# Splitting a tile's new weights: all quarters on VectorE, one per tick, instead of two on VectorE and two on GpSimd

## The chip, the cores and the metric

One core of a Trainium2 chip. The metric is the time of one execution in microseconds of the device; a time of a kernel is the median of several executions.

## The reference

Three layers over 10112 tokens (2 sequences of 5056) of width 256. The first is a linear recurrence along each sequence, the other two are mixtures of 8 experts of which each token takes one.

```python
# recurrence, per channel
log_a = 8 * sigmoid(r_gate) * log(clip(sigmoid(a_param)))
a = exp(log_a);  g = sqrt(max(1 - a*a, 1e-6)) * sigmoid(i_gate) * x
h[t] = a[t] * h[t-1] + g[t]
# mixture of experts; the second layer has no modality bias
logits = x @ w_gate + modality_bias[modality_id]
e = argmax(logits);  gate = softmax(logits)[e]
out = gate * (max(x @ w1[e], 0) @ w2[e])      # w1 256 x 1024, w2 1024 x 256
```

## The kernel before

**Tiles and slots.** A layer's tokens are sorted by expert: each is given a row number and GpSimd scatters its row to memory by an indirect DMA (`scatter`, L217). A *tile* is 256 rows of one expert. The program has a fixed sequence of *slots*, one tile each: slots 0 to 39 are layer 1, slots 40 and later layer 2. Which expert a slot's tile has, and whether its weights differ from those that its weight set holds, is worked out on the chip in tables (`plan_steps`) and read from there by each engine as a register (`entry`).

**Arithmetic.** TensorE takes 32-bit numbers in a form that holds only part of their digits, so every operand stands as two parts, high and low: `w1h, w1l, w2h, w2l` for weights, `xh, xl` for the tile's rows, `hTh, hTl` for the hidden layer. A product is three matmuls: high by high, low by high, high by low (`ffn1`, L898 to L900; `ffn2`, L912 to L914). ScalarE makes `hTh` (L902), VectorE `hTl` (L903).

**Ticks.** A slot is 6 ticks (`POINTS`): `ffn1` in ticks 0 to 3, `ffn2` in ticks 4 and 5. The main loop (L1110 to L1152) issues a tick's matmuls and then, in turn with one another, the steps that the agenda holds for that tick: chunks of the recurrence (`chunk_at`, layer 1 only), the routing (`pick`, `rank`), the list of a later phase's tiles (`plan_steps`), and what follows the slot before (`end_steps`). Every engine runs its own queue in program order.

**Weights.** There are two sets of weights on chip, which slots use in turn. SyncE loads a later slot's w1 and w2 as four quarters of 128 x 1024 into buffers named `stage` (`load_weights`, L798 to L817). `split` (L857 to L881) makes two parts of a quarter: ScalarE copies it to the high part (L863), then the difference is taken as the low part (L864) by the engine that a letter names, V for VectorE and G for GpSimd. Quarters 0 and 1 are w1, 2 and 3 are w2. In layer 1 a small fifth piece, `stagew` (128 x 64, always VectorE), holds columns that give the second layer's routing. All of it is under a condition (`when`, a test and a jump on each engine that takes part) on the table's entry `f2`, except in the first two slots of a layer, whose weights always change. A slot of which the condition holds is called a *reload* here.

```python
POINTS = 6
SPLIT = (4, 4, 5, 5)                     # tick in which each quarter of the next slot's weights is split
BY = ('VVVG', 'VVGG', 'VVGG')            # engines: first tile, slot 0, other slots
parts = [i for i in range(4) if SPLIT[i] == point]                      # in the main loop
split(nxt, *parts, *([4] if 3 in parts and t else []), by=BY[1 if t == 0 else 2])
```

So both w1 quarters are split behind the last hTl of a slot, in tick 4, and both w2 quarters in tick 5. `maybe_steps` (L1041 to L1080) holds the slots of layer 1 that may stay empty, as a nest of conditions; VectorE's test for the first of them is at L1063. `other_gates` (L847 to L855) has a jump at L852.

Of the kernel before, what the change touches and what calls it, by code (L numbers as in the profile page):

```python
# [16 lines left out]
P = 128  # L17
E = 8
# [4 lines left out]
T = 256  # tokens of a tile  # L23
H = T // P
CH = 512  # steps of the scan in a chunk
W = D + 2  # a row for a layer: token, its number, its gate
WR = D + E
GP = 128  # columns of the products with the second layer's gates
BIG = float(1 << 22)
CUTS = (1, 2, 3, 4, 6, 8)  # chunks of the scan after which tiles are listed  # L30
SW_QUEUES = 8
POINTS = 6  # ticks of a slot
SPLIT = (4, 4, 5, 5)  # ticks of a slot in which the quarters of the next one's weights are split
AHEAD = 11  # ticks from a chunk's loads to its start
T0 = 45
START = (5, 15, 34)
GATE = (3, 5)  # ticks of the first slot at which the gates of its and the next one's experts are worked out
FIRST = (37, 38, 45, 46)  # ticks of the splits of the first tile's weights
LOAD2 = T0 + 4
PACE = 12  # ticks between chunks, at least  # L40
NPH = 3
BIAS = 1
# Ticks of a chunk's steps, from its start: for the first, the second, the third, and the rest.
# [23 lines left out]
LISTS = (4, 4, 4, 4, 8)  # ticks that the phases' lists take  # L67
LATE = 4
BY = ('VVVG', 'VVGG', 'VVGG')  # engines that split the weights' quarters, of the first slots and the others
WARM = ((0, 'r', 1, 4, 2), (0, 'i', 1, 8, 2), (0, 'q', 1, 10, 3))  # products that keep TensorE's clock up: chunk, what they read, tick, how many  # L70
ALIGN = (0, 5)  # tick of a slot at which a chunk starts
# [10 lines left out]
def token_tiles(B, S):  # L82
    """Chunks of the scan (first step, steps, first token tile, token tiles), and the token tiles:
    lists of (sequence, first step, steps)."""
    chunks, tiles = [], []
    s = 0
    while s < S:
        w = min(CH, S - s)
        mine = []
        for b in range(B):  # L90
            for j in range(w // P):
                mine.append([(b, s + j * P, P)])
        rest = w % P
        if rest:
            assert rest * B == P
            mine.append([(b, s + w - rest, rest) for b in range(B)])
        chunks.append((s, w, len(tiles), len(mine)))
        tiles += mine
        s += w
    return chunks, tiles  # L100


LEAD = 4  # slots between the second layer's first list and its first tile


def phases(B, S):
    """How the tiles of both layers are cut into phases: (layer, routed chunks or slots that a
    phase's list rests on, slots, slots that are always run, last of the layer, first slot among
    those that are always run). Whatever the experts' shares, n routed tokens fill
    (n - E (T - 1)) / T tiles; the first phases have slots for as many as two experts' shares fill,  # L110
    and a slot that finds no tile runs on padding."""
# [6 lines left out]
    full = 0  # tiles done for certain  # L118
# [22 lines left out]
def positions(slots, filled, t):  # L141
    """Places in a phase's list, slot by slot: two runs side by side, as there are two sets of
    weights on chip; slots that may stay empty come last."""
    evens = len([i for i in range(filled) if (t + i) % 2 == 0])
    n = [0, evens]
    res = []
    for i in range(filled):
        res.append(n[(t + i) % 2])
        n[(t + i) % 2] += 1
    return res + list(range(filled, slots))  # L150


def shape_consts(B, S):
    """Arrays that depend on the shapes alone."""
# [20 lines left out]
def pair(a):  # L175
    """The two halves of a token tile's logits, innermost."""
    return bass.AP(a.tensor, a.offset, [list(a.ap[0]), [1, E], [D + E, 2]])


def scan_moe_moe2(tc, xT, rT, iT, apar, mod, mbias, wg1, wg2, wA1, wB1, wA2, cst_d, ids_d, tab_d, out):  # L180
# [11 lines left out]
    with ExitStack() as st:  # L192
# [12 lines left out]
        # Rows that experts get are written once, each to a place of its own, and read by tiles of  # L205
        # later phases: the accesses to them need no order but that of a phase behind its writes.
# [69 lines left out]
        # 4 * log(clip(sigmoid(a))): half of the decay's factor  # L276
# [19 lines left out]
        # the modality's bias of every token, by exact selection  # L296
# [17 lines left out]
        # rows that pad an expert's last tile: zeros, with a token number out of range  # L314
# [3 lines left out]
        # ... and a tile of them, for slots that find none  # L318
# [7 lines left out]
        def weave(a, b):  # L326
            """Two lists of steps as one, evenly."""
# [11 lines left out]
        def pick(lg, n, mk):  # L339
            """Of logits lg [P, n, E], in steps: the one-hot of the first maximum (bf16), and the  # L340
            softmax's value there."""
# [15 lines left out]
        def rank(oh, n, bs, mk, place):  # L357
            """In steps: the row numbers of n tiles' tokens behind `bs`, which moves on past them."""
# [33 lines left out]
        def at(tick, f, early=False):  # L392
            """Has a step done at a tick, among those of TensorE before the tile's or among the rest."""
            agenda.setdefault(tick, ([], [], []))[0 if early else 1].append(f)

        def at_all(tick, f):
            """Has the steps that `f` returns done at a tick, in turn with others."""
            agenda.setdefault(tick, ([], [], []))[2].append(f)

        def chunk_at(ci, s, first):  # L400
            """A chunk's steps from tick s on; a step's inputs are there by then, so that it doesn't
            hold up its engine."""
# [95 lines left out]
            def warm(box_, n_):  # L498
                """Products that nobody needs, which keep TensorE's clock up while it waits for the scan."""
# [30 lines left out]
        done = {}  # L530
        tabs = {}
        have = cp.tile([1, E], F32, name="have")  # whether an expert's gates are known
# [3 lines left out]
        def plan_steps(pi):  # L536
            """Lists a phase's tiles: expert, first row, whether the weights change, whether there
            is one."""
# [154 lines left out]
        def fresh(pi):  # L693
            """Whether a phase finds other weights on chip than its layer's."""
            return pi == 0 or plans[pi][0] != plans[pi - 1][0]

# [1 line left out]
        main = [(pi, s) for pi, pl in enumerate(plans) for s in range(pl[3])]  # L698
        NS = len(main)
        xT_, hT, pos = {}, {}, {}  # L700

        class Ring:
            """Buffers that tiles take in turn. While `held`, those at hand go round, as what is done
            under a condition can't get tiles."""
# [30 lines left out]
        class Slot:  # L735
            """A place for one tile: its phase and its place there, its set of weights, its buffers."""

            def __init__(self, pi, s, ws, pool_, bufs, tag=""):
# [4 lines left out]
                self.v = None  # L743
# [3 lines left out]
            def t(self, n):  # L747
                """A tile of this slot, got when first asked for."""
# [26 lines left out]
        def guard(sl):  # L775
            """For what is done for a slot only if there is a tile for it."""
# [21 lines left out]
        def load_weights(sl, part, gates=True):  # L798
            wA = wA1 if sl.layer == 1 else wA2
            if part == 0:  # L800
                sl.ev = sl.entry(0, {ET.SP}, E - 1)
                sl.f = None if sl.always else sl.entry(1, {ET.SP}, 1)
            js = {0: (0, 1), 1: (2, 3), 2: ()}[part]
# [19 lines left out]
        def gate(w, ps_, out):  # L823
            """w2  w_gate, of an expert whose w2 is in w, transposed."""
# [22 lines left out]
        def other_gates(sl):  # L847
            """All experts' gates, if a phase needs others than are known."""
# [7 lines left out]

        def split(sl, *parts, by=BY[2]):  # L857
            """Weights in two parts that TensorE takes in one pass each, a quarter at a time."""
# [20 lines left out]
            if 0 in parts and not sl.always:  # L879
# [36 lines left out]
        def end_steps(sl):  # L916
            """What follows a tile's products, in six parts."""
# [36 lines left out]
        slots = [Slot(pi, s, t % 2, mp, (3, 5)) for t, (pi, s) in enumerate(main)]  # L954

        # Ticks: those of the head, then POINTS of every slot. When chunks start: at the shortest
        # distance as long as there are no tiles, then in time for the lists that rest on them.
# [45 lines left out]
        def early(upto):  # L1003
            """The steps of TensorE at the tick before `upto`, and all before them."""
# [6 lines left out]
        def later(upto, *others):  # L1011
            """All steps of the ticks before `upto`, in turn with others."""
# [22 lines left out]
        for i, tick in enumerate(FIRST):  # L1035
            at(tick, lambda i=i: split(slots[0], i, by=BY[0]), early=True)
# [4 lines left out]
        def maybe_steps(pi):  # L1041
            """The first layer's slots that may stay empty, one by one: what is loaded for the first
            ahead of time, and all."""
# [38 lines left out]
        def tail(sl, nxt, nx2, rest):  # L1082
            """The second layer's slots that may stay empty, each with the start of the one behind."""
# [24 lines left out]
        prev = nest = None  # L1108
        todo = []
        for t, sl in enumerate(slots):  # L1110
# [8 lines left out]
            for point in range(POINTS):  # L1119
                early(tick(point))  # L1120
# [14 lines left out]
                if nxt:  # L1135
                    parts = [i for i in range(4) if SPLIT[i] == point]
                    if parts:
                        split(nxt, *parts, *([4] if 3 in parts and t else []), by=BY[1 if t == 0 else 2])
# [66 lines left out]
```

## Time and profile before

| | us |
|---|---|
| median of 3 runs | 1214.02 |
| lowest, highest run | 1210.79, 1217.70 |
| span of the profiled execution, first to last instruction | 1190.4 |
| TensorE busy in it | 1088.4 (91%), mean granted clock 0.962 |
| VectorE busy | 672.5 (56%) |
| ScalarE busy | 511.2 (43%) |
| GpSimd busy | 382.1 (32%) |

The profile is of one execution, whose own time from outside is not recorded; its span covers the instructions alone, and the medians contain what lies before and after them as well. PE is TensorE's matmuls, PEld its weight loads (in parallel with PE), DVE is VectorE, ACT ScalarE, POOL GpSimd, SP SyncE; a q behind an engine's name is its sequencer. "L864" is a line of the kernel before. Idle time of an engine is shown with what ended it.

### The profile page before, as it was taken

Reading aid. Unit: us, or ns where it says so; the run is one execution under the profiler, and the core shown is the slowest. Engines: PE = TensorE matmul, PEld = TensorE weight load, DVE = VectorE, ACT = ScalarE, POOL = GpSimd, SP = SyncE. Lnnn points to the kernel's source line nnn. Section 1 sums busy time; section 2 is a strip of 40 time slices with the busy share of each in tenths; the row PEclk is TensorE's granted clock in tenths of the full one; section 3 lists DMA queues with packets and bytes.
Section 4 is the critical chain, followed back from the end, with each engine's and each line's share of the span. In section 5 each row is a group of like instructions: output and inputs, shape, how many; then the busy total and the mean of one; then the engine's idle time right before and its main releaser. Section 6 shows DMA issues by size and latency. Waiting matters only on the chain. (4 is left out here: it accounts for less than half of the span.)

```text
span 1190.4 us, 26921 instructions
## 1 busy us (share of the span) xinstructions
PE 1088.4 (91%) x9112; PEld 1073.5 (90%) x9112; DVE 672.5 (56%) x1954; ACT 511.2 (43%) x817; POOL 382.1 (32%) x414
## 2 busy tenths in 40 slices
PE   4287889897999899989999799999999999999997
PEld 2287889897999899979999799999999999999997
DVE  6768778978686848555456643332434443333352
ACT  7735557546273525223234323332434542224362
POOL 2417341466241514241112421311333531113152
PEclk9688989998999989999999899999999999999999
DMA  7764464364333212151114233113332431113350
GB/s 248 236 226 147 169 180 134 109 215 162 114 113 108 96 46 74 41 140 50 37 55 140 77 119 120 43 50 108 122 108 73 141 120 47 45 53 106 124 171 26
DMA packets 69236, 133.76 MB, mean 112 GB/s; under 512 B 9740, under 2 KB 37395, under 8 KB 69042
## 3 DMA queue, kind: packets, MB, share of 16 engines
q1 hardware_dynamic: 57186, 100.19, 26.9%
q0 software_dynamic: 11856, 31.25, 7.4%
q8 instruction: 89, 1.46, 0.5%
q14 instruction: 105, 0.86, 0.2%
HBM read 95.49 MB, written 37.03 MB: 111 GB/s over the span
## 5 line engine op out<-in xcount | busy, mean ns | idle before, releaser
L912 PE MATMUL po<-w2h,hTh 128*128 128x256 f32 (+1 forms) x1344 | 396.1, 295 | 4.9 <-PEq L852 3.4
L898 PE MATMUL ph<-xh,w1h 128*128 128x256 f32 x1312 | 374.6, 286 | 26.8 <-DVEq L1063 7.9
L913 PE MATMUL po<-w2l,hTh 128*128 128x256 f32 (+1 forms) x1344 | 385.2, 287 | 1.1 <-DVE w2l L864 1.1
L914 PE MATMUL po<-w2h,hTl 128*128 128x256 f32 (+1 forms) x1344 | 384.7, 286 | 0.7 <-DVE hTl L903 0.7
L899 PE MATMUL ph<-xl,w1h 128*128 128x256 f32 x1312 | 370.1, 282 | 4.6 <-DVE xl L889 4.6
L900 PE MATMUL ph<-xh,w1l 128*128 128x256 f32 x1312 | 370.1, 282 | 1.2 <-DVE w1l L864 1.2
L903 DVE SCALAR_TENSOR_TENSOR hTl<-ph,hTh 128x512 fp32r<-128x512 f32 x336 | 231.2, 688 | 210.5 <-ACT hTh L902 208.9
L902 ACT ACTIVATE hTh<-ph 128x512 fp32r<-128x512 f32 x336 | 199.0, 596 | 321.7 <-PE ph L900 310.4
L898 PEld LDWEIGHTS ph<-xh,w1h 128*128 128x128 f32 x1312 | 252.4, 192 | 28.6 <-issue 15.6
L912 PEld LDWEIGHTS po<-w2h,hTh 128*128 128x128 f32 x1344 | 259.6, 193 | 3.6 <-issue 3.6
L913 PEld LDWEIGHTS po<-w2l,hTh 128*128 128x128 f32 x1344 | 259.5, 193 | 2.9 <-issue 1.6
L914 PEld LDWEIGHTS po<-w2h,hTl 128*128 128x128 f32 x1344 | 258.8, 193 | 1.1 <-DVE hTl L903 1.1
L899 PEld LDWEIGHTS ph<-xl,w1h 128*128 128x128 f32 x1312 | 250.5, 191 | 4.8 <-DVE xl L889 4.8
L900 PEld LDWEIGHTS ph<-xh,w1l 128*128 128x128 f32 x1312 | 249.8, 190 | 1.6 <-DVE w1l L864 1.6
L217 POOL DMA_INDIRECT out_dram<-orow,xr x88 | 86.5, 983 | 283.9 <-ACT orow L924 237.5
L924 ACT ACTIVATE orow<-po,xr 128x256 f32<-128x256 f32 x124 | 58.0, 472 | 274.8 <-PE po L914 272.6
L217 POOL DMA_INDIRECT X<-orow,rib x80 | 80.7, 1008 | 184.9 <-DVE rib L951 64.0
L864 POOL TENSOR_TENSOR w2l<-stage,w2h 128x1024 fp32r<-128x1024 f32 x37 | 93.3, 2542 | 127.8 <-ACT w2h L863 127.8
L929 DVE TENSOR_SCALAR orow<-po,xr 128x256 f32<-128x256 f32 x44 | 21.3, 484 | 148.8 <-PE po L914 148.8
L217 POOL DMA_INDIRECT X<-row,ria x79 | 88.4, 1119 | 23.6 <-issue 15.9
L459 PE MATMUL ps<-wI,it 128*128 128x136 f32 x280 | 49.0, 301 | 19.3 <-DVE it L438 15.5
L459 PEld LDWEIGHTS ps<-wI,it 128*128 128x128 f32 x280 | 39.8, 200 | 21.6 <-ACT rt L411 11.1
(171 smaller groups left out, 1044.1 us busy)
## 6 DMA issues: line engine op xcount, KB each, us to landing
stage<-in_wA SPq DMA_DIRECT2D x76, 512.0 KB, 4.6
xr<-X SPq DMA_DIRECT2D x84, 258.0 KB, 2.8
rt<-in_rT SPq DMA_DIRECT2D x18, 512.0 KB, 4.9
it<-in_iT SPq DMA_DIRECT2D x18, 512.0 KB, 5.5
xt<-in_xT SPq DMA_DIRECT2D x18, 512.0 KB, 4.7
X<-zr SPq DMA_DIRECT2D x17, 258.0 KB, 3.6
it<-in_wB SPq DMA_DIRECT2D x4, 512.0 KB, 7.8
out_dram<-orow,xr POOLq DMA_INDIRECT x88, 2.4
```

The costliest lines, as they stand in the source:

```text
L217: i = G.indirect_dma_start(out=dst, out_offset=bass.IndirectOffsetOnAxis(ap=idx, axis=0), in_=rows, in_offset=None, bounds_check=bound, oo ...
L459: PE.matmul(p[:, k * (P + E):(k + 1) * (P + E)], l[:, k, :], wI[:, k, :], start=True, stop=True)
L864: by.tensor_tensor(out=l, in0=src, in1=h.bitcast(F32), op=ALU.subtract)
L898: PE.matmul(p[:, j, :], h1[:, k, cs], sl.t("xh")[:, k, :], start=k == 0, stop=False)
L899: PE.matmul(p[:, j, :], h1[:, k, cs], sl.t("xl")[:, k, :], start=False, stop=False)
L900: PE.matmul(p[:, j, :], l1[:, k, cs], sl.t("xh")[:, k, :], start=False, stop=k == KD - 1)
L902: A.activation(hh[:], p[:], func=ACTF.Relu)
L903: V.scalar_tensor_tensor(out=hl[:], in0=p[:], scalar=0.0, in1=hh[:].bitcast(F32), op0=ALU.max, op1=ALU.subtract)
L912: PE.matmul(p[h][:, :wd], hh, h2[:, c, :wd], start=c == 0, stop=False)
L913: PE.matmul(p[h][:, :wd], hh, l2[:, c, :wd], start=False, stop=False)
L914: PE.matmul(p[h][:, :wd], hl, h2[:, c, :wd], start=False, stop=c == KF - 1)
L924: A.activation(orow[:, h, :D], p[h][:, :D], func=ACTF.Copy, scale=g1[:, h:h + 1])
```

## The change

All four quarters are split on VectorE; only the first tile of the program keeps its last quarter on GpSimd. The quarters go to ticks 2, 3, 4 and 5 of a slot, one each, where their loads were issued at least `LOADED` = 4 ticks before; otherwise to the ticks of before (`SPLIT_LATE`). For that, `load_weights` notes at which tick each half was issued. The table's entry `f2` is read at a slot's first split instead of at that of quarter 0. The rest of the diff takes comments away, so that line numbers of the changed kernel differ by a few.

```diff
-SPLIT = (4, 4, 5, 5)
+SPLIT = (2, 3, 4, 5)
+SPLIT_LATE = (4, 4, 5, 5)
+LOADED = 4
-BY = ('VVVG', 'VVGG', 'VVGG')
 ...
+        now = [-POINTS]
 ...
-                self.v = None
+                self.v = self.f2 = None
 ...
             if part == 0:
                 sl.ev = sl.entry(0, {ET.SP}, E - 1)
                 sl.f = None if sl.always else sl.entry(1, {ET.SP}, 1)
+                sl.came = {}
+            sl.came[part] = now[0]
 ...
-        def split(sl, *parts, by=BY[2]):
+        def split(sl, *parts, by='VVVV'):
 ...
-            if 0 in parts and not sl.always:
+            if sl.f2 is None and not sl.always:
                 sl.f2 = sl.entry(1, {ET.Activation, ET.DVE, ET.Pool}, 1)
 ...
-            at(tick, lambda i=i: split(slots[0], i, by=BY[0]), early=True)
+            at(tick, lambda i=i: split(slots[0], i, by='VVVG'), early=True)
 ...
             for point in range(POINTS):
+                now[0] = t * POINTS + point
 ...
-                    parts = [i for i in range(4) if SPLIT[i] == point]
+                    when_ = lambda i: SPLIT[i] if t * POINTS + SPLIT[i] >= nxt.came.get(i // 2, 1 << 20) + LOADED else SPLIT_LATE[i]
+                    parts = [i for i in range(4) if when_(i) == point]
                     if parts:
-                        split(nxt, *parts, *([4] if 3 in parts and t else []), by=BY[1 if t == 0 else 2])
+                        split(nxt, *parts, *([4] if 3 in parts and t else []))
```

How this moves instructions is seen best on VectorE. In its queue the number of tests on a register (COMPARE_AND_BRANCH) goes from 226 to 373, in ScalarE's from 233 to 380, in GpSimd's from 226 to 373; TensorE and SyncE keep theirs. The unconditional jumps are at the ends of the conditions' bodies.

VectorE in slot 3, from its last hTl on; w1l, w2l are the low parts, stage the loaded quarters, xl the next tile's rows, pbb the routing's; TENSOR_LOAD and ISA read the table's entry. Before:

```order
L903 SCALAR_TENSOR_TENSOR hTl<-ph,hTh 128x512
L889 TENSOR_TENSOR xl<-pt,xh 128x512
L773 TENSOR_LOAD tj_1016
L773 ISA x2
L787 COMPARE_AND_BRANCH
L864 TENSOR_TENSOR w1l_159<-stage,w1h_158 128x1024 x2
L787 UNCONDITIONAL_BRANCH x3
L787 COMPARE_AND_BRANCH
L864 TENSOR_TENSOR w2l_161<-stagew,w2h_160 128x8x8
L787 UNCONDITIONAL_BRANCH x3
L373 TENSOR_TENSOR pbb<-ph,base_152 128x16
```

With the change:

```order
L907 SCALAR_TENSOR_TENSOR hTl<-ph,hTh 128x512
L893 TENSOR_TENSOR xl<-pt,xh 128x512
L789 COMPARE_AND_BRANCH
L868 TENSOR_TENSOR w1l_159<-stage,w1h_158 128x1024
L789 UNCONDITIONAL_BRANCH x2
L789 COMPARE_AND_BRANCH
L868 TENSOR_TENSOR w2l_161<-stage,w2h_160 128x4x256
L789 UNCONDITIONAL_BRANCH x4
L789 COMPARE_AND_BRANCH
L868 TENSOR_TENSOR w2l_161<-stage,w2h_160 128x4x256
L868 TENSOR_TENSOR w2l_161<-stagew,w2h_160 128x8x8
L789 UNCONDITIONAL_BRANCH x2
```

One w1 quarter stands here instead of two, each w2 quarter follows under a test of its own, and the table's entry has been read earlier; pbb and what follows it come behind all of this.

VectorE in slot 12, from its third hTl to its last; the operations on gb, big, bg, dn are the routing's and the next list's. Before:

```order
L903 SCALAR_TENSOR_TENSOR hTl<-ph,hTh 128x512
L352 TENSOR_REDUCE gb<-exb 128x2
L605 TENSOR_SCALAR dn_4980<-exc 1x8
L353 TENSOR_SCALAR gb<-gb 128x2
L616 TENSOR_TENSOR big<-big,bg_4970 1x64
L354 RECIPROCAL gb<-gb 128x2
L609 SCALAR_TENSOR_TENSOR dn_4980<-dn_4980,av 1x8
L417 SCALAR_TENSOR_TENSOR it<-it,xt 128x512
L619 TENSOR_TENSOR bg_4970<-big,tab 1x64
L903 SCALAR_TENSOR_TENSOR hTl<-ph,hTh 128x512
L889 TENSOR_TENSOR xl<-pt,xh 128x512
```

With the change:

```order
L907 SCALAR_TENSOR_TENSOR hTl<-ph,hTh 128x512
L775 TENSOR_LOAD tj_3542
L775 ISA x2
L789 COMPARE_AND_BRANCH
L868 TENSOR_TENSOR w1l_163<-stage,w1h_162 128x1024
L789 UNCONDITIONAL_BRANCH x2
L353 TENSOR_REDUCE gb<-exb 128x2
L606 TENSOR_SCALAR dn_4998<-exc 1x8
L354 TENSOR_SCALAR gb<-gb 128x2
L617 TENSOR_TENSOR big<-big,bg_4988 1x64
L355 RECIPROCAL gb<-gb 128x2
L610 SCALAR_TENSOR_TENSOR dn_4998<-dn_4998,av 1x8
```

The table's entry is read here now, and the first w1 quarter stands ahead of all that leads to the last hTl of the slot.

## Rows read from the trace of the kernel before

**Rows 1.** The page, busy time by engine.
```profile
PE 1088.4 (91%) x9112; PEld 1073.5 (90%) x9112; DVE 672.5 (56%) x1954; ACT 511.2 (43%) x817; POOL 382.1 (32%) x414
```

**Rows 2.** Busy time by stretch: us, PE, PEld, DVE, ACT, POOL busy, PEclk, DMA share, GB/s.
```profile
157.00:272.00 115.00, 103.86 (x869) 102.17 (x868) 93.31 (x328) 63.19 (x95) 43.44 (x60) 0.93 0.49 157
...
677.00:1172.00 495.00, 494.31 (x4202) 493.73 (x4200) 196.36 (x304) 181.71 (x296) 143.59 (x111) 1.00 0.30 95
```

**Rows 3.** Waits of TensorE: us in total, times, longest.
```profile
PE ph L898 <- DVE hTl L903: 6.7, 3, 5.7
...
PE pt L887 <- DMA xr<-X: 0.5, 1, 0.5
```

**Rows 4.** The instructions of L864 on each engine: ns min/median/max, first and last start.
```profile
L864 DVE TENSOR_TENSOR w1l<-stage,w1h x38: 1199/1219/1227, 47.0 to 1157.2; 128x1024 fp32r<-128x1024 f32 x38
L864 POOL TENSOR_TENSOR w2l<-stage,w2h x37: 2339/2418/2947, 63.5 to 1160.6; 128x1024 fp32r<-128x1024 f32 x37
```

**Rows 5.** Timeline, end of slot 0: start, us, engine, line, instruction [idle before <-releaser].
```profile
72.29 0.39 PE L913 MATMUL po<-w2l,hTh 128*128 128x264 f32 x1 [1.10 <-DVE w2l L864]
```

**Rows 6.** Timeline from the end of slot 0, GpSimd and VectorE.
```profile
88.61 5.29 POOL L864 TENSOR_TENSOR w2l<-stage,w2h 128x1024 fp32r<-128x1024 f32 x2 [22.57 <-ACT w2h L863]
...
88.62 2.46 DVE L584 TENSOR_TENSOR big<-av,tab 1x64 f32<-1x64 f32 x1
...
91.85 2.06 DVE L590 TENSOR_TENSOR exc<-inc,av 1x8 f32<-1x8 f32 x1
...
96.07 0.68 DVE L903 SCALAR_TENSOR_TENSOR hTl<-ph,hTh 128x512 fp32r<-128x512 f32 x1
```

**Rows 7.** Timeline from the end of slot 3, GpSimd, VectorE and TensorE.
```profile
137.99 4.76 POOL L864 TENSOR_TENSOR w2l<-stage,w2h 128x1024 fp32r<-128x1024 f32 x2 [4.85 <-ACT w2h L863]
...
139.03 1.46 DVE L864 TENSOR_TENSOR w2l<-stagew,w2h 128x64 fp32r<-128x64 f32 x1 [1.75 <-ACT w2h L863]
...
140.82 2.01 DVE L378 TENSOR_TENSOR pb<-pb,oh 128x64 f32<-128x64 f32 x1
142.75 0.16 DVE L378 TENSOR_TENSOR pbb<-pbb,ohb 128x16 f32<-128x16 f32 x1
...
145.84 0.58 PE L898 MATMUL ph<-xh,w1h 128*128 128x256 f32 x1 [3.20 <-DVE cnt L561]
```

**Rows 8.** Busy time by stretch, columns as in the second group.
```profile
144.80:151.50 6.70, 5.66 (x26) 5.66 (x27) 6.56 (x32) 5.14 (x7) 5.47 (x6) 0.50 0.38 91
295.40:298.20 2.80, 2.80 (x13) 2.80 (x14) 2.68 (x12) 1.07 (x3) 0.99 (x1) 0.50 0.01 3
406.00:412.00 6.00, 4.69 (x38) 4.52 (x39) 5.86 (x28) 3.12 (x6) 3.48 (x4) 1.00 0.24 86
```

**Rows 9.** Timeline from the end of slot 12, VectorE and TensorE.
```profile
288.12 2.29 DVE L613 TENSOR_TENSOR dn<-dn,dn 1x8 f32<-1x8 f32 x1
...
291.02 2.35 DVE L628 TENSOR_TENSOR bg<-bg,big 1x64 f32<-1x64 f32 x1
...
295.29 0.55 PE L898 MATMUL ph<-xh,w1h 128*128 128x256 f32 x1 [5.71 <-DVE base L376]
```

**Rows 10.** Timeline at the end of slot 39, VectorE, ScalarE and TensorE.
```profile
653.56 2.08 DVE L378 TENSOR_TENSOR pbb<-pbb,ohb 128x16 f32<-128x16 f32 x1
...
655.88 2.04 DVE L951 TENSOR_TENSOR rib<-rb,vbb 128x2 int32<-128x2 f32 x1
...
655.34 0.47 ACT L924 ACTIVATE orow<-po,xr 128x256 f32<-128x256 f32 x1 [0.94 <-PE po L914]
...
663.22 0.55 PE L898 MATMUL ph<-xh,w1h 128*128 128x256 f32 x1 [7.92 <-DVEq L1063]
```

**Rows 11.** Timeline of VectorE in slot 11, behind a jump.
```profile
269.12 0.69 DVE L417 SCALAR_TENSOR_TENSOR it<-it,xt 128x512 f32<-128x512 f32 x1 [0.45 <-DVEq L787]
```

**Rows 12.** Timeline of GpSimd in slot 1, scatters.
```profile
103.27 1.91 POOL L217 DMA_INDIRECT X<-row,ria  x1 [0.30 <-issue]
105.48 0.97 POOL L217 DMA_INDIRECT X<-row,ria  x1 [0.30 <-issue]
```

More of the change, by code (lines that the diff above doesn't have):

```diff
@@ L1108, in scan_moe_moe2 @@
         prev = nest = None
+        now[0] = 0
         todo = []
```

## The prediction, made before the changed kernel was run

> **What bounds the kernel now.** I read the page first. TensorE is busy 91% of the span [rows 1], so time can be won only where TensorE stands still or runs at a lower clock. Next I read busy time by stretch: from 677 to 1172 us, nearly all of layer 2, TensorE is busy 494.31 of 495 us at a granted clock of 1.00 [rows 2], although eleven of the 18 reloads lie there. Nothing can be won in that stretch; what is added there must only stay hidden. The waits of TensorE put the rest before 677 us: 6.7 us in three waits for hTl, the longest 5.7 [rows 3], one of 5.71 for base [rows 9], one of 7.92 behind VectorE's sequencer at L1063 [rows 10]. What these have in common is seen in the timelines [rows 6, 7, 9, 10]: ahead of each, small VectorE operations last 2 us where their like last 0.15 to 0.2, exactly while GpSimd splits.
>
> So the question is what the six reloads of layer 1 (in slots 0, 1, 3, 10, 12 and 39) cost today through GpSimd, and what the same work costs on VectorE.
>
> **The prices.** A quarter takes 1.22 us on VectorE and 2.42 on GpSimd [rows 4]. GpSimd has 37, and keeps that of the first tile: 36 × 2.42 = 87 us leave it, and 36 × 1.22 = 44 us come to VectorE. In each reload VectorE gains two quarters, 2.4 us, and loses the lengthened operations. I take the reloads one by one. Every instant is one of the profiled execution, whose span is 1190.4 us; if its whole time is the median of the runs, 1214.0, then 23.6 us lie outside the span. What comes off the span I take off the median.
>
> **Slots 0 and 1.** In slot 0 the first w1 quarter moves ahead of the slot's last hTl. TensorE waits there already, 1.10 us until 72.29, for the stagew piece that VectorE does right behind that hTl [rows 5]. There is no slack, so 1.2 us are lost. At the end of the slot GpSimd's two quarters (5.29 us from 88.61) go, and with them the lengthening of big (2.46 us) and exc (2.06) [rows 6]; their like take 0.21 and 0.15, so 2.25 + 1.9 = 4.15 us are freed. From big at 88.62 to hTl at 96.07 it is 7.45 us, in the new order 3.3. GpSimd begins when the first copied quarter is there; VectorE can begin its one quarter at that point too, 1.2 later by the stall, at 89.8, and ends it at 91.0. Four small operations (0.9 us) and the 3.3 follow: hTl at 95.2, or 95.6 if something else slips. Both slots together give +0.5 to +0.9; I take **+0.7**. TensorE still stands over 4 us there.
>
> **Slots 3 and 4.** GpSimd works from 137.99 to 142.75; in it w2l<-stagew takes 1.46 us, and pb 2.01 where pbb right after takes 0.16 [rows 7]. Without the second alone, the hTl for which TensorE waits until 145.84 (its row names cnt, next behind hTl) comes 1.8 us earlier. Besides, ScalarE's first copy moves two ticks ahead into idle time, so that its last one ends about 1 us earlier, and VectorE's two quarters fit into the 1.75 us that it idles today before the stagew piece: that piece then ends near 139.3 instead of 140.5. Together 3.0, less 0.3 for two more conditions. Bounds 1.8 and 3.0; I take **+2.5**. The stall of 3.20 us shrinks to 0.7. After it the granted clock is 0.50 until 151.5 [rows 8], the lower of the two levels, 1.2 instead of 2.4 GHz: 26 matmuls take 5.66 us there, 0.22 each, where 4202 take 494.31 in layer 2, 0.12 each. Where TensorE stood still for 1.3 of 6 us, from 406 on, it stayed at 1.00 [rows 8]. So the half clock after 145.84 may go: 26 times 0.1 is 2.6 us. It may stay, or the time be lost again to VectorE, which is busy 6.56 of 6.70 us there. I take less than half, **+1.0**, with bounds 0 and 2.6.
>
> **Slot 10.** No wait of TensorE ends on this reload: 0.
>
> **Slots 12 and 13.** While GpSimd splits, dn takes 2.29 and bg 2.35 [rows 9], 4.3 us more than their like. Two quarters, 2.4 us, come to VectorE. The w1 quarter that moves ahead of hTl leaves this chain by as much as it delays what stands before it; two short waits of TensorE for w1l go, and the last products of slot 12 start later instead. base, which lets TensorE go on at 295.29, gains 4.3 − 2.4 = 1.9, less 0.3 for conditions: bounds +1.0 and +1.9, I take **+1.5**.
>
> **Slot 39.** pbb (2.08) and rib (2.04) are lengthened [rows 10], by 3.8 us. VectorE's branch of L1063 stands shortly behind rib, and TensorE starts 5.3 us after rib's end. Two quarters come in, 2.4 us, and one w1 quarter, 1.2, goes ahead: 3.8 − 2.4 + 1.2 = 2.6. But ScalarE's last orow ends at 655.8, and VectorE's work on it follows: with the same 5.3 us TensorE can't start before 661.1, so 2.1 at most. Bounds +1.2 (some of the quarter ahead is not gained) and +2.0, I take **+1.5**.
>
> **The conditions.** Each quarter mostly gets a condition of its own: VectorE's and ScalarE's queues have 147 more tests each. Where the weights stay, an engine jumps over the piece. Such a jump shows as 0.45 us of idle time before VectorE's next operation [rows 11]. Two more jumps in 34 slots of layer 1 are 68, but VectorE idles in most of them. They reach TensorE where it waits for VectorE with no reload near; I find five such places in its list of waits. Five times 0.3; bounds 0 and 4.5 (ten jumps at 0.45). I take **−1.5**. In layer 2 I take 0: the cover is that VectorE is busy 196.36 of 495 us there [rows 2], so that 7 us of each 11.8 us slot are free for 2.4 more. Without that cover a reload there would cost 2.4 us.
>
> **The sum.** 0.7 + 2.5 + 1.0 + 1.5 + 1.5 − 1.5 = 5.7 us: a span of 1184.7, and 1214.0 − 5.7 = **1208.3 us**. All low bounds give 0.5 + 1.8 + 0 + 1.0 + 1.2 − 4.5 = 0, all high ones 0.9 + 3.0 + 2.6 + 1.9 + 2.0 = 10.4: 1204 to 1214.
>
> **The rivals.** *The holding turns round.* VectorE's quarters hold up GpSimd too: a scatter's descriptors took 1.91 us beside a w1 quarter, and 0.97 right after it [rows 12]. With 12 quarters more on VectorE in the six reloads, scatters lose up to 12 × 0.94 = 11 us on GpSimd, and later loads wait for their rows. For it: scatters stand one behind the other there. Against it: the same reloads free 12 × 2.42 = 29 us of GpSimd, and TensorE waits for loaded rows once, 0.5 us [rows 3]. If one such delay in each reload reached TensorE, 5.6 us of the gain would go: 1214.
>
> The Trainium skill speaks to this (SBUF — State Buffer, section "SBUF: two separate sides"): VectorE and GpSimd share a pair of ports that whichever starts first holds for its whole instruction, among others a VectorE operation with two SBUF inputs against a GpSimd one that reads SBUF; and it warns that GpSimd, locked out, cannot write descriptors. The trace agrees in the lengthened rows, and for a scatter with 0.94 us more; a block for a quarter's whole 1.22 us would make it 15 us on GpSimd instead of 11.
>
> *Nothing moves.* VectorE is itself the bound in these stretches (6.56 of 6.70 us behind 144.8 [rows 8], and 2.4 more come into each reload), so the quarters fill what the blocks free: the low bounds, 1214.
>
> *Slower: the jumps.* The place is VectorE's queue in the layer-1 slots without a reload, where steps of the scan, the routing and hTl stand behind each jump. If one of the two new jumps in each of 34 slots reaches TensorE at 0.45 us, that is 15.3 us against gains of 7.2: 1222. It decides from 16 jumps on (7.2 / 0.45). For it: VectorE is busy 93.31 of 115 us from 157 on [rows 2]. Against it: TensorE waits for VectorE at a handful of places only, and is busy 103.86 of those 115 us.
>
> *More: the clock.* It is at half behind 295.29 too, where 13 matmuls take 2.80 us [rows 8]. If that stall also ends before the clock falls, its stretch gives 1.3, and slot 4's its whole 2.6: 5.7 + 1.3 + 1.6 = 8.6, 1205, and less still if the same holds in slot 1. Against it: by my sum both stalls stay near 4 us.
>
> That the change does less than it says is no rival: in VectorE's order the w2 quarters stand in every reload, and the first w1 quarter ahead of the last hTl.
>
> **How the numbers follow.** A measurement of this kernel tells 0.5%, 6.07 us, from no change: under 1207.95 is faster, over 1220.1 slower. The forecast's own case has 0.48; as its centre lies at the edge, that is 0.22 faster and 0.26 same. The clock has 0.20, all faster. Nothing moves has 0.14 and the holding 0.05, all same. The jumps have 0.13, 0.10 of it slower and 0.03 same. Faster 0.42, same 0.48, slower 0.10. The range, 1201 to 1218, holds the forecast's 1204 to 1214 and the clock's case with some scatter of the runs (before they lie 3 to 4 us about their median), and leaves out the jumps.
>
> **What would show it.** Right: no VectorE operation of 2 us in the places of [rows 6, 7, 9, 10]; the stalls at 145.84, 295.29 and 663.22 smaller by 2.5, 1.5 and 1.5, the one at 72.29 larger by 1.2; TensorE still without gaps in layer 2. Wrong: new waits of TensorE behind VectorE in slots without a reload (the jumps), scatters of 1.9 us that a load waits for (the holding), or gaps in layer 2, where I have none.

## The result, and the profile after

| | before | with the change |
|---|---|---|
| median of 20 runs, us | 1211.27 (1202.19 to 1217.99) | 1199.94 (1192.39 to 1209.28) |
| ratio, 95% interval | | 0.9911 (0.9892 to 0.9931) |
| span of the profiled execution, us | 1190.4 | 1199.8 |

The change makes the kernel 0.9% faster, where 0.47% was forecast; 1199.94 us lies just under the range of 1201 to 1218. The profiled execution after it is longer than the one before; the section on the reasons argues from their traces that the two were taken on chips on which the kernel takes different times.

The page after the change, busy time by engine (answers to [rows 1]):

```profile
span 1199.8 us, 27555 instructions
...
PE 1094.6 (91%) x9112; PEld 1075.5 (90%) x9112; DVE 688.7 (57%) x1990; ACT 513.8 (43%) x817; POOL 297.3 (25%) x378
```

GpSimd loses 85 us of work, VectorE gains only 16: 44 came in, and some 28 us went, most of it the lengthening of small operations. The instructions of the split after the change (answers to [rows 4]; ns min/median/max, first and last start):

```profile
L868 DVE TENSOR_TENSOR w1l<-stage,w1h x38: 1204/1216/1226, 47.9 to 1167.2; 128x1024 fp32r<-128x1024 f32 x38
L868 DVE TENSOR_TENSOR w2l<-stage,w2h x37: 1199/1218/1237, 60.8 to 1169.5; 128x1024 fp32r<-128x1024 f32 x37
L868 DVE TENSOR_TENSOR w2l<-stagew,w2h x6: 206/217/228, 75.0 to 304.7; 128x64 fp32r<-128x64 f32 x6
L868 POOL TENSOR_TENSOR w2l<-stage,w2h x1: 2542/2542/2542, 65.3 to 65.3; 128x1024 fp32r<-128x1024 f32 x1
```

The stagew piece, 1.46 us in [rows 7], is never over 0.23 now. VectorE's timeline after the change, slot 3 and slot 12 into 13 (answers to [rows 7, 9]):

```profile
145.18 0.21 DVE L379 TENSOR_TENSOR pb<-pb,oh 128x64 f32<-128x64 f32 x1
145.32 0.17 DVE L379 TENSOR_TENSOR pbb<-pbb,ohb 128x16 f32<-128x16 f32 x1
...
302.48 0.13 DVE L614 TENSOR_TENSOR dn<-dn,dn 1x8 f32<-1x8 f32 x1
...
303.23 0.21 DVE L629 TENSOR_TENSOR bg<-bg,big 1x64 f32<-1x64 f32 x1
303.54 1.20 DVE L868 TENSOR_TENSOR w2l<-stage,w2h 128x1024 fp32r<-128x1024 f32 x1
```

pb takes 0.21 for 2.01, dn 0.13 for 2.29, bg 0.21 for 2.35: no small VectorE operation of layer 1 lasts over 0.7 us any more. TensorE's timeline, the first matmul after each stall (answers to [rows 7, 9, 10]):

```profile
148.40 0.39 PE L902 MATMUL ph<-xh,w1h 128*128 128x256 f32 x1 [0.47 <-DVE cnt L562]
...
306.48 0.55 PE L902 MATMUL ph<-xh,w1h 128*128 128x256 f32 x1 [4.20 <-DVE base L377]
...
672.17 0.55 PE L902 MATMUL ph<-xh,w1h 128*128 128x256 f32 x1 [5.56 <-DVEq L1067]
```

3.20 us have become 0.47, 5.71 have become 4.20, 7.92 have become 5.56: less by 2.7, 1.5 and 2.4, where 2.5, 1.5 and 1.5 were forecast. These are single executions: in a second trace of the kernel before (E0 below) the last two are 4.55 and 7.03. Busy time by stretch, layer 2 and what follows the first of these stalls (columns as in [rows 2]):

```profile
687.00:1182.00 495.00, 494.29 (x4203) 493.91 (x4203) 218.51 (x329) 182.90 (x296) 92.83 (x87) 1.00 0.30 95
148.40:156.00 7.60, 6.85 (x52) 6.07 (x52) 7.35 (x41) 6.35 (x9) 5.84 (x8) 1.00 0.56 146
```

Layer 2 is as full as before with 22 us more on VectorE, and the granted clock stays at 1.00 behind the short stall, where it was 0.50 behind the long one [rows 8].

### The profile page after: what moved, and what is told of

Read it like the earlier page. It is cut to its first block, busy times and chain, and to the rows that moved or that the text cites. A ratio compares the mean times of both kernels' runs of the same rounds, so it can differ in the third digit from the quotient of the medians.

```text
span 1199.8 us, 27555 instructions
## 1 busy us (share of the span) xinstructions
PE 1094.6 (91%) x9112; PEld 1075.5 (90%) x9112; DVE 688.7 (57%) x1990; ACT 513.8 (43%) x817; POOL 297.3 (25%) x378
## 5 line engine op out<-in xcount | busy, mean ns | idle before, releaser
L218 POOL DMA_INDIRECT out_dram<-orow,xr x88 | 93.8, 1065 | 409.8 <-ACT orow L928 362.4
L893 DVE TENSOR_TENSOR xl<-pt,xh 128x512 fp32r<-128x512 f32 x82 | 55.7, 680 | 1.2 <-ACT xh L892 0.6
```

The costliest lines, as they stand in the source:

```text
L218: i = G.indirect_dma_start(out=dst, out_offset=bass.IndirectOffsetOnAxis(ap=idx, axis=0), in_=rows, in_offset=None, bounds_check=bound, oo ...
L893: V.tensor_tensor(out=sl.t("xl")[:], in0=p[:], in1=sl.t("xh")[:].bitcast(F32), op=ALU.subtract)
```

## The experiments

Runs of one group were measured on one chip, against runs of the kernel before on the same chip.

**Which half: the engine or the ticks.** E0 is the kernel before, E3 the changed one, each again. E1 takes the engine alone, E2 the ticks alone:

```diff
# E1, from the kernel before
-BY = ('VVVG', 'VVGG', 'VVGG')
+BY = ('VVVG', 'VVVV', 'VVVV')
# E2, from the changed kernel: in the slots that may stay empty, and in the main loop
-split(sl, 0, 1, 2, 3, 4)
+split(sl, 0, 1, 2, 3, 4, by='VVGG')
 ...
-split(nxt, *parts, *([4] if 3 in parts and t else []))
+split(nxt, *parts, *([4] if 3 in parts and t else []), by='VVGG')
```

> The kernel before, unchanged, for a second profile. The profiled execution of before had a span of 1190.4 us, while the 20 runs have a median of 1211.3 and a lowest of 1202.2; for the changed kernel span and time of the profiled execution differ by 1.9 us. If the profile that the prediction rests on was an uncommonly short execution (theory A), this span is 1200 to 1216, and the surplus over 1190 shows up as longer stalls of TensorE at places in layer 1. If a fixed 20 us lies outside the span (theory B, which the prediction took), the span is again near 1190. Ratio 1.000 either way.

> All quarters on VectorE, but at the ticks of before (4, 4, 5, 5), with the conditions of before. If what is won comes from taking the splits off GpSimd, so that VectorE's small operations are no longer lengthened (theory E, engine), the ratio is 0.990 to 0.995 and no small VectorE operation of 2 us is left. If it comes from the ticks (theory T), the ratio is 0.998 to 1.005, as four quarters (4.9 us) then stand in one lump ahead of the next slot's first hTl.

> The new ticks (2 to 5, one quarter each, with their conditions), but w2 still on GpSimd (VVGG). Theory E: VectorE's small operations stay lengthened while GpSimd splits, now over a wider stretch, ratio 0.998 to 1.006. Theory T: ratio 0.990 to 0.995.

> The changed kernel, unchanged, for a second profile and a direct comparison on the same chip as the two halves of the change. Ratio 0.989 to 0.993 as measured. If the sum of the prediction holds (theory E), the stalls of TensorE at the ends of slots 3, 12 and 39 are again near 0.5, 4.2 and 5.6 us.

Measured, with before at 1203.87 us: E0 0.9995 (0.9972 to 1.0019), E1 0.9920 (0.9895 to 0.9946), E2 1.0025 (1.0013 to 1.0037), E3 0.9901 (0.9878 to 0.9925). The engine is what gains; the ticks with their conditions, but without it, lose. E0's span is 1202.9, its time 1204.67: theory A, nothing of 20 us lies outside the span. In E1 no VectorE operation of layer 1 that writes at most 64 columns takes over 0.5 us, where in the trace of before ten take over 1.5. In E2 the lengthening is still there:

```profile
140.15 2.03 DVE L379 TENSOR_TENSOR pb<-pb,oh 128x64 f32<-128x64 f32 x1
142.10 0.16 DVE L379 TENSOR_TENSOR pbb<-pbb,ohb 128x16 f32<-128x16 f32 x1
```

This is VectorE's timeline of E2 behind slot 3: the rows of before, 2.01 and 0.16 [rows 7], once more.

**Where, and through what.** E4 and E5 put VectorE into the reloads of slots 0 to 39 and of slots from 40 on alone. E6 gives each quarter a condition of its own and changes nothing else. E7 leaves the work on GpSimd but cuts each quarter into four instructions.

```diff
# E4 (E5: t >= 40), from the kernel before
-split(nxt, *parts, *([4] if 3 in parts and t else []), by=BY[1 if t == 0 else 2])
+split(nxt, *parts, *([4] if 3 in parts and t else []), by='VVVV' if t < 40 else 'VVGG')
# E6
-if parts:
-    split(nxt, *parts, *([4] if 3 in parts and t else []), by=BY[1 if t == 0 else 2])
+for i in parts:
+    split(nxt, i, *([4] if i == 3 and t else []), by='VVGG')
# E7, where the engine is GpSimd
-by.tensor_tensor(out=l, in0=src, in1=h.bitcast(F32), op=ALU.subtract)
+for c in range(4):
+    G.tensor_tensor(out=l[:, c], in0=src[:, c], in1=h[:, c].bitcast(F32), op=ALU.subtract)
```

> Kernel before with VectorE for all quarters in the six reloads of slots 0 to 39 only; old ticks, GpSimd as before in layer 2. If all of the gain is lengthened VectorE operations ahead of stalls in layer 1 (theory E), the ratio is that of the version with VectorE everywhere at the old ticks, 0.990 to 0.995. If part of it comes from layer 2 or from a program that is lighter on GpSimd throughout (theory S), it is 0.995 to 0.999.

> The other half: VectorE for all quarters from slot 40 on only. Theory E and the prediction: TensorE has no gaps there, ratio 0.999 to 1.001. Theory S: 0.994 to 0.998.

> Kernel before with a condition of its own for each quarter, same ticks and engines: the tests and jumps of the change alone. The prediction priced them at 1.5 us with bounds 0 and 4.5: ratio 1.000 to 1.004. The rival of the jumps said 15 us: 1.012. If more tests also mean more stalls on instructions that are not there yet, 1.004 or more.

> Kernel before with each of GpSimd's quarters as four instructions of a quarter of the columns: GpSimd's work stays the same or grows a little, but no single instruction lasts over about 0.7 us. If VectorE's small operations wait for the end of one GpSimd instruction (theory E), those of 2 us become 0.3 to 0.9, and the ratio is 0.994 to 0.998. If what matters is that GpSimd is busy and late with what is behind the split (theory S), the ratio is 0.999 to 1.004.

Measured, with before at 1208.83: E4 0.9928 (0.9901 to 0.9954), E5 0.9978 (0.9958 to 0.9997), E6 1.0031 (1.0011 to 1.0050), E7 0.9963 (0.9945 to 0.9981). Most of the engine's gain is in the six reloads of layer 1, as theory E has it. E5 gains a little that theory E does not explain; it lies in the range of theory S. Nearly all its slots of layer 2 take 11.74 to 11.78 us as before, but slot 42 does not: it takes 13.27 us in E4, 13.08 in E6 and 12.02 in E5. GpSimd ahead of that slot, then TensorE in it, in E4, whose layer 2 is that of before:

```profile
685.62 5.03 POOL L864 TENSOR_TENSOR w2l<-stage,w2h 128x1024 fp32r<-128x1024 f32 x2 [3.32 <-ACT w2h L863]
691.47 0.99 POOL L217 DMA_INDIRECT X<-orow,rib  x1 [0.82 <-POOL w2l L864]
...
706.59 0.66 PE L887 MATMUL pt<-cst,xr 128*128 128x128 f32 x4 [1.25 <-DMA xr<-X]
```

and in E5:

```profile
696.06 0.98 POOL L217 DMA_INDIRECT X<-orow,rib  x1 [7.67 <-ACT hTh L902]
...
711.43 0.66 PE L887 MATMUL pt<-cst,xr 128*128 128x128 f32 x4
```

TensorE waits for rows (xr) that a load brings from where GpSimd scattered them, and in E4 the last scatters of X stand behind GpSimd's two quarters. In E5 they go out 1.5 us earlier, counted from the start of slot 42 (699.51 in E4, 705.60 in E5), and the wait is gone. All eight traces with GpSimd's splits in layer 2 have this wait, of 0.48 to 1.57 us; in the twelve with VectorE it is 0.56 at most and mostly absent. The wait itself is measured; that it goes because GpSimd is free earlier is read from these rows and was not tried by itself. It is some 1.1 of E5's 2.7 us (its interval goes from 0.4 to 5.1); what else there is stays open.

E7 tells best what the mechanism is: the same work on the same engine, in shorter instructions, wins about half of what E4 wins on the same chip by moving it. Its VectorE timeline, slot 13:

```profile
297.53 0.63 DVE L613 TENSOR_TENSOR dn<-dn,dn 1x8 f32<-1x8 f32 x1
298.09 0.16 DVE L685 CAST tj<-tb 1x24 int32<-1x24 f32 x1
298.17 0.67 DVE L434 TENSOR_TENSOR it<-it,qt 128x512 f32<-128x512 f32 x1
298.77 0.76 DVE L628 TENSOR_TENSOR bg<-bg,big 1x64 f32<-1x64 f32 x1
```

and the pieces on GpSimd, all 148:

```profile
L866 POOL TENSOR_TENSOR w2l<-stage,w2h 128x256 fp32r<-128x256 f32 x148 | 114.8, 811 | 129.4 <-ACT w2h L863 111.3 <-DMA stage<-in_wA 18.0
```

GpSimd is busy 114.8 us with them, more than the 93.3 of the 37 whole quarters in the trace of before, and the kernel is faster all the same. dn and bg wait 0.5 to 0.6 us for a piece where they waited 2.2 for a quarter [rows 9]: a VectorE operation that is held mostly waits for the end of one GpSimd instruction. That agrees with the Trainium skill (SBUF — State Buffer, section "SBUF: two separate sides"), by which the one that starts first holds the shared ports for its whole instruction. It does not always get its turn between two of them: at the end of slot 1, in the trace of before, GpSimd's two quarters and the stagew piece on VectorE are

```profile
106.71 4.71 POOL L864 TENSOR_TENSOR w2l<-stage,w2h 128x1024 fp32r<-128x1024 f32 x2
...
107.36 4.15 DVE L864 TENSOR_TENSOR w2l<-stagew,w2h 128x64 fp32r<-128x64 f32 x1
```

so that this piece, 0.21 us by itself, was held to the end of both.

**Ticks and conditions.** E8 is E1 with a condition for each quarter, that is, the change without its ticks. E9 takes early ticks without more conditions, two quarters in tick 3 and two in tick 4. E10 has VectorE in slot 12's reload alone. E11 is the change with the ticks of before in slot 0.

```diff
# E8, from E6, with E1's BY
-    split(nxt, i, *([4] if i == 3 and t else []), by='VVGG')
+    split(nxt, i, *([4] if i == 3 and t else []), by='VVVV')
# E9, from the changed kernel
-SPLIT = (2, 3, 4, 5)
+SPLIT = (3, 3, 4, 4)
# E10, as E4 but for the last argument
+... by='VVVV' if t == 12 else 'VVGG')
# E11, from the changed kernel
-when_ = lambda i: SPLIT[i] if t * POINTS + SPLIT[i] >= ...
+when_ = lambda i: SPLIT[i] if t and t * POINTS + SPLIT[i] >= ...
```

> All quarters on VectorE at the old ticks, each under a condition of its own: the changed kernel without its ticks. Theory E with ticks worth nothing (the prediction's sum: -1.2 us in slot 0, about +1.2 in slot 4): ratio as the changed kernel, 0.989 to 0.992. Theory ET (engine and ticks add up): VectorE at old ticks gave 0.992 and own conditions 1.003, so 0.995, and the ticks alone are worth 0.005 of the changed kernel's 0.990.

> The changed kernel with two quarters per tick, w1 in tick 3 and w2 in tick 4 (ticks 4 and 5 where loads came late): earlier than before, but with no more tests than before. If the added tests cost 0.003 and early splitting is worth 0.003 to 0.005 with VectorE (theory ET), this is 0.985 to 0.989, the shortest so far. If only one quarter at a time helps, it is 0.990 to 0.994.

> Kernel before with VectorE for w2 in the single reload of slot 12. The prediction's term is +1.5 us plus the 0.3 for conditions that are not there: ratio 0.9985, bounds 0.998 to 0.999. If this term is what was too small (its slots 12 and 13 took 38.4 and 45.4 us in two traces of before and 34.3 to 36.4 with VectorE): 0.994 to 0.997.

> The changed kernel with the ticks of before in slot 0 alone. The wait of TensorE for the stagew piece, 2.64 us in the traces of the changed kernel and 1.1 to 1.5 before, goes back to 1.1 to 1.5, as no quarter stands ahead of the last hTl. If that reaches the end, as the prediction has it (1.2 us): 0.001 under the changed kernel's ratio of 0.990; if what follows in slots 0 and 1 waits for something else: the same ratio.

Measured, with before at 1192.19: E8 0.9974 (0.9958 to 0.9990), E9 0.9923 (0.9903 to 0.9942), E10 0.9981 (0.9966 to 0.9995), E11 0.9924 (0.9902 to 0.9945). E10 is 2.3 us, near the forecast's term of 1.5 and 0.3. E9 missed theory ET: early ticks without the added tests are no shorter than the change (E11, which differs from it in slot 0 alone). In E11 TensorE's wait for the stagew piece is gone; a gain of 0.001 is too small for its interval to show or exclude. In the traces none is seen: slots 0 and 1 take 58.28 us in E11 and 57.05 to 61.86 in four traces of the change, and TensorE stands 4.43 us for hTl at the end of them, where those have 3.4 to 5.6.

**All parts on one chip.** E12, E13, E14 and E15 are E1, E6, E8 and the changed kernel again.

> VectorE for all quarters, old ticks, old conditions, now on the same chip as the next three. Theory ET: 0.991 to 0.994. If the engine's part was a matter of the chip of the first measurement: over 0.995.

> Own conditions alone, GpSimd as before. Theory ET: 1.002 to 1.005. If the first measurement showed only how that chip delivers instructions: 0.999 to 1.001.

> Both, old ticks. Theory ET (they add): 0.994 to 0.998, between the two before it. If conditions cost nothing: as VectorE alone.

> The changed kernel on this chip. Theory ET: 0.989 to 0.992, so that the ticks alone are worth 0.004 to 0.006 against the kernel with both at the old ticks. If the ticks are worth nothing: as that kernel.

Measured, with before at 1192.21: E12 0.9931 (0.9906 to 0.9956), E13 1.0003 (0.9987 to 1.0020), E14 0.9970 (0.9952 to 0.9989), E15 0.9927 (0.9900 to 0.9953). The engine is worth 0.0069 (8.2 us), conditions of their own beside it cost 0.0039 (4.6 us), and the ticks give that back: 0.0043 (5.1 us). The last two are differences of ratios whose intervals touch. For the ticks, E8 and E11 (0.9974 and 0.9924) say the same on one other chip; for the conditions there is no second pair on one chip. The parts do not simply add, as theory ET had it: E13, the conditions beside GpSimd's splits, missed its 1.002 to 1.005 and costs nothing that can be told from noise, though E6 cost 0.0031 on another chip. One place that the ticks may act on is VectorE's waits behind its own sequencer's jumps (us in total, times, longest), in E12

```profile
DVE it L417 <- DVEq L787: 1.8, 4, 0.5
```

in E14

```profile
DVE it L417 <- DVEq L787: 5.3, 5, 1.4
...
DVE it L438 <- DVEq L787: 4.9, 10, 0.8
...
DVE pbb L373 <- DVEq L787: 4.1, 9, 0.5
```

and in E15

```profile
DVE it L418 <- DVEq L789: 3.9, 5, 1.1
...
DVE pbb L374 <- DVEq L789: 0.8, 2, 0.5
```

Over all such rows VectorE idles 3.1 us behind jumps in E12, 21.5 in E14 and 7.2 in E15; but also 13.7 in E13, which loses nothing, so the idle time by itself is not the cost. At the old ticks the added jumps stand ahead of the scan and the routing (it, pbb) in a row; spread over the ticks most of them show no idle time of their own. That they are then hidden in waits for ScalarE is likely, but was not tried by itself, and how they reach the end is not shown. Nor do the ticks give the time back where the conditions took it: slots 5 to 9 take 88.4 us in E12, 91.1 in E14 and 91.5 in E15.

**Is there a better one, and does the chip matter.** E16 is E9 and E17 the changed kernel, beside each other.

> Two quarters per tick (w1 in tick 3, w2 in tick 4), no added tests, beside the changed kernel on one chip. If the added tests are what the changed kernel pays for its ticks (theory ET: 0.004), and pairs keep the ticks' gain, this is 0.003 to 0.005 under the changed kernel. If one quarter per tick is what gains, both come out the same within 0.002, at 0.990 to 0.993.

> The changed kernel, for the comparison with the pairs: 0.989 to 0.993. On a chip on which the kernel before takes over 1200 us (instructions late in slots 10 to 28) 0.989 to 0.991, on one with 1192 us 0.992 to 0.993, if late instructions explain why the ratio differs between chips.

Measured, with before at 1204.54: E16 0.9877 (0.9846 to 0.9909), E17 0.9885 (0.9853 to 0.9917). Pairs at early ticks without added tests do as well as the change, not better. No version beat it clear of noise, and the simplest, the engine alone, can't be told from it: 0.9931 and 0.9927 on one chip (E12, E15), 0.9920 and 0.9901 on another (E1, E3).

## Why the prediction was right in its mechanism and wrong in its number

**The steps that failed: the base, and the size of three terms.** The prediction said: "if its whole time is the median of the runs, 1214.0, then 23.6 us lie outside the span. What comes off the span I take off the median." It is not: in the profiled executions of E0 to E17 time and span differ by 1.7 to 2.1 us. So the execution shown of before took some 1192 us, what the kernel takes on the chips of E8 to E15, while the runs shown lie about 1211. What the chips over 1200 us have more shows in the list of waits. VectorE ahead of hTl and ScalarE ahead of hTh, in E0:

```profile
DVE hTl L903 <- ACT hTh L902: 168.9, 221, 7.3
DVE hTl L903 <- issue: 53.0, 37, 3.0
...
ACT hTh L902 <- issue: 17.1, 16, 2.7
```

in the profile shown of before:

```profile
DVE hTl L903 <- ACT hTh L902: 208.9, 250, 8.2
...
ACT hTh L902 <- issue: 1.1, 1, 1.1
```

and in the profile after the change:

```profile
DVE hTl L907 <- ACT hTh L906: 159.1, 201, 7.7
DVE hTl L907 <- issue: 52.7, 36, 3.4
...
ACT hTh L906 <- issue: 9.2, 6, 2.7
```

"issue" is time in which the engine waited for nothing that the profile shows. hTl has 45 to 54 us of it in the traces from chips on which the kernel before takes 1204 us or more (E0 to E7, E16, E17, and the profile after), and none in those from chips at 1192 (E8 to E15, and the profile shown of before). Where it falls on layer 1, slots grow: slot 12 takes 12.7 us in the trace of before and 19.8 in E0's. No record names the chips of the two profiles shown; that they are of different kinds is read from this row and their spans. So sum and time were taken from two kinds of chip, and a stall that the prediction never saw was part of the time it started from. The stall is as long with the change (52.7 us): it goes with the longer base, while its total does not explain a larger gain; where it falls may.

Of the 8.4 us by which 1199.94 lies under 1208.3, 2.8 are the base itself, as the three runs shown had a median of 1214.0 and the twenty one of 1211.3. The other 5.6 are the gain, 11.3 us for 5.7. On the chip of E12 to E15 the change gains 8 to 9, so about 3 us are terms that were too small: slots 10 to 13, slot 39 and layer 2, in the table below. The rest, nearly 3, is seen only on chips of the other kind, and as the intervals of the ratios overlap it is not sure.

**The sum, against a trace of the same kind.** The forecast span was 1184.7 us; E15's is 1182.6, on a chip of the kind that the rows came from. Time between the first matmuls of slots, in us:

| slots | before | E15 | gain | forecast |
|---|---|---|---|---|
| 0, 1 | 57.45 | 57.49 | 0.0 | +0.7 |
| 3, 4 | 30.39 | 26.75 | +3.6 | +2.5 and +1.0 |
| 5 to 9 | 88.38 | 91.54 | −3.2 | −1.5 for all conditions |
| 10 to 13 | 65.69 | 62.93 | +2.8 | +1.5 |
| 14 to 38 | 332.54 | 332.07 | +0.5 | |
| 39, 40 | 33.82 | 31.00 | +2.8 | +1.5 |
| from 41 on | 513.56 | 512.21 | +1.4 | 0 |

With slot 2 and the start that is 7.8 us for 5.7. Each is one execution; the same program can differ by 1 to 2 us in such a row, and by more in slots 0 and 1.

- *Layer 2 stays full*: right, 494.29 of 495 us. *Nothing can be won there*: wrong by about 1 us, the wait for xr in slot 42 (E5); its line stood in [rows 3], and the prediction used it only against a rival.
- *The lengthening goes with GpSimd's splits*: right, by E1, E2 and E7. The engine without conditions and ticks was forecast at about 7.8 us (5.7, 1.5 and 0.6 for conditions, slot 0's 1.2 less 1.2 for ScalarE's early copy) and measured 8.2; that the two agree so well is in part luck, as single terms were off both ways.
- *Slots 3 and 4, clock*: right in its parts. The stall of 3.20 us is 1.35 to 1.39 with the engine alone (E1, E4, E12), 1.8 less as forecast, and 0.47 with the ticks too, 0.9 less for a forecast 1.2 less 0.3. Busy time by stretch in E15, behind the stalls of 0.47 and 4.08 us: the granted clock stays at 1.00 behind the first and is 0.50 behind the second.

```profile
143.00:151.00 8.00, 7.06 (x53) 6.28 (x54) 7.75 (x42) 6.76 (x9) 6.22 (x9) 1.00 0.57 148
292.60:298.00 5.40, 5.36 (x25) 5.39 (x26) 5.24 (x22) 2.13 (x4) 2.55 (x3) 0.50 0.14 49
```

- *Slots 10 to 13 and slot 39*: right in sign, low by half.
- *Slot 0*: the wait for the stagew piece grew as said, from 1.10 to 2.64 us in E15; that it reaches the end was not seen (E11).
- *Conditions*: mis-sized. 1.5 us were forecast from five places at 0.3; beside VectorE's splits they cost 4.6 (E12, E14), beside GpSimd's nothing clear of noise on the same chip (E13).
- *Ticks*: taken as an even trade, they are worth 5.1 once the conditions are there. These two errors cancel, which is luck.

**The rivals.** *The jumps* exist, but cost a third of their 15 us. *The holding turned round* is visible and harmless; one row each of the pages of E0 and of the change, scatters of layer 2 (count, busy us, mean ns):

```profile
L217 POOL DMA_INDIRECT out_dram<-orow,xr x88 | 86.6, 984 | 284.7 <-ACT orow L924 238.2
```

```profile
L218 POOL DMA_INDIRECT out_dram<-orow,xr x88 | 93.8, 1065 | 409.8 <-ACT orow L928 362.4
```

A scatter takes 0.08 us more, and GpSimd has 125 us more idle time before them. The mean hides the few that are held: in E15 17 scatters run beside a quarter on VectorE (by over 0.1 us) and take 1.55 us on average, the other 230 take 1.04. That is some 9 us of GpSimd's time in the whole program, where the forecast's bound was 11 for six reloads, and no wait of TensorE for loaded rows is left in E15. The warning about descriptors that the prediction took from the Trainium skill (SBUF — State Buffer, section "SBUF: two separate sides") is given there for VectorE operations in a two-port mode, which a subtraction of two tensors does not have; that such a subtraction goes with longer scatters is what this trace shows. *Nothing moves* is out. *More: the clock* (1205) came nearest in time, but not by its mechanism: the clock in slot 13 still falls.

**What stays open.** The change gives 0.9927 on a chip at 1192 us and 0.9885 to 0.9911 on those at 1204 to 1211, so 2 to 5 us of its gain may belong to the second kind; the intervals of E15 and E17 overlap. In their traces slots 10 to 13 take 76.1 us in E0, 72.5 in E5 and 73.5 in E6, and 64.7 to 68.1 with the change or its pairs (E3, E16, E17). The halves on the chip of E0 point to the engine, 65.6 in E1 against 75.1 in E2; but E4, with VectorE in layer 1, has 71.7 on another, and each is one execution. What the chips differ in no run tells. As each chip was used for one group of runs only, it is not shown either that it is the chip and not the occasion.

## What to carry to other kernels

When two engines read on-chip memory, price an operation not only by its own length but by what it does to the other engine's small operations: here 2.4 us instructions on an "idle" engine cost more on the bound one than doing the work there, and cutting them short was worth about half of moving them. Where the moved work goes, look also at what stood behind it in the old engine's queue: scatters went out 1.5 us earlier. A test and a jump can cost anything from nothing to 4.6 us for 147 of them, by what stands beside them: measure it in place. Before a sum is taken off a median, check that the profiled execution belongs to it: 24 us between span and time, at an expected 2, was the sign here.

## What the hardware showed that was not expected

- The same program took 1192 us in two groups of runs and 1204 to 1211 in the four others, and the difference goes with one row, hTl behind "issue": 45 to 54 us or none.
- A held VectorE operation mostly waits for one GpSimd instruction and not for its whole burst (0.6 to 0.8 us long in E7, 2.0 to 2.5 before), but one was held 4.15 us, to the end of two.
- A VectorE quarter holds a scatter in turn: 1.55 us beside one, 1.04 otherwise (E15).
- The granted clock stayed at 1.00 behind a stall of 0.47 us and was at 0.50 behind stalls of 3.20 and 4.08.
